# A banded attention with a squared-ReLU expert layer: the values of all head pairs in plain float32, two heads in the two column halves of the array

## The chip, the cores and the metric

The kernel runs on one core of one Trainium2 chip. The metric is the device time of one execution in microseconds (us). Of a time, three runs are shown: 820.58 us at the median, from 820.32 to 820.78.

A core has five engines with queues of their own. PE (TensorE) multiplies matrices: one operand is loaded into its array as weights (the profile calls these loads PEld), the other streams through, and the result goes to PSUM, a small memory of eight banks with 512 float32 columns each. DVE (VectorE) and ACT (ScalarE) work on SBUF and on PSUM, POOL (GpSimd) on SBUF alone, and SP issues the DMAs. An operand has up to 128 partitions (rows); "128*64 128x256" in a row of the profile says that 128 rows and 64 columns of the array are used and that the moving operand has 128 partitions and 256 columns.

## What is computed

```python
def _attn_ref(q, k, v, n_sink, window):          # q, k, v: (4, 8, 768, 64) float32
    scores = np.matmul(q, k.transpose(0, 1, 3, 2)) / np.sqrt(D)
    is_sink = pos[None, :] < n_sink               # n_sink = 4
    rel = pos[:, None] - pos[None, :]
    keep = is_sink | ((rel >= 0) & (rel < window))  # window = 128
    scores = np.where(keep, scores, -1e9)
    a = np.exp(scores - scores.max(-1)); a = a / (a.sum(-1) + 1e-9)
    return np.matmul(a, v)

x = attn_out.transpose(0, 2, 1, 3).reshape(3072, 512)
h = np.maximum(x @ w_in, 0.0)                     # w_in (512, 2048), w_out (2048, 512), float64
out = (h * h @ w_out).astype(np.float32)
```

Each query sees at most its window of 128 keys and the first four keys, the sinks.

## The kernel before

**Tiles.** The 3072 tokens are eight chunks of 384 queries, two to a batch (a first half and a second half). The eight heads go as four pairs, so there are 32 pairs of chunk and heads, numbered 0 to 31. A query block of 128 sees its own key block, the one before it and 8 sink columns that are kept beside every key block. A first-half pair has three key blocks, a second-half pair four. A key block that two query blocks see is "wide" (256 columns of queries), one that a single query block sees is "thin" (128). In a first-half pair only the last query block needs sink columns (128); in a second-half pair all three do (384).

**Two ways to multiply float32.** The format float32r goes through the array in one pass, with a rounded operand. To keep accuracy, a value is split into a rounded part and the rest (hi and lo), and the products are added up. Plain float32 needs no split and leaves two matmul records in the trace for one product. Scores of pairs 0 to 5 (`NPS`) and values of pairs 0 to 7 (`NPV`) are plain; all others, and the expert layer, go as hi and lo.

**A slot** handles the scores of pair s, the values of pair s-1 and the operands of pair s+1. `score` makes a product (L235 plain, L239 split), the masking with the maximum on DVE (L243), the exponential on ACT (L246), and at the end of a head DVE makes the reciprocal of the sums (L249, L250), POOL scales the probabilities (L253) and copies their sink columns together (L257, tile `PSk`). `sink_keys` transposes these (L265) and copies them out of PSUM. `probs` transposes the probabilities into three PSUM banks (L311): the wide blocks of head 0, the thin blocks of both heads, the wide blocks of head 1. For a split pair ACT makes the hi part (L329, L334) and DVE the rest (L330, L335); for a plain pair one copy does (L317 on DVE, L319 on ACT). `values` multiplies with v (L365) and with the sinks' v (L378 plain with 16 rows, L386 split with 48 rows). A split product has v's hi part in array columns 0 to 63 and its lo part in 64 to 127, so the upper and lower halves of the result must be added: L393 to L396. Then x is split for the expert layer (L382, L383 or L397, L398). A plain product uses columns 0 to 63 alone, for both heads, one after the other. The result tile `xo` is one PSUM bank. v of a split pair is itself split by DVE and POOL (L209, L210), the sinks' v by DVE (L180, L181).

**The expert layer** (`moe`) goes per chunk through 16 blocks of 128 hidden columns: twelve products of 384 columns into `ph` (L458), ReLU on ACT (L466, tile `r`), the square once as hi on ACT (L470, `gh`) and once in full on DVE (L471), the rest `gl` on DVE (L472). Nine products of 512 columns with w_out (L485) follow one block later, into three PSUM banks that collect all blocks of a chunk. `ph` has two banks.

**Weights** come as float64 and are turned into hi and lo on DVE, ACT and POOL by `split_part` (L542 to L554), row by row, between the other work of the first 230 us. For this the first two chunks' products go by halves of the weights.

**Order.** The program is written as one list of units. A planner (the tile framework) turns it into the queue of each engine by the order of the text, its priorities and estimated costs; a block under `tc.manual_schedule` keeps the written order on the named engines. Each engine then works through its queue in order and waits at semaphores. In slots without expert products before them (pairs 0 to 4) the attention goes beside the weights; then each step of the expert layer is followed by its share of attention units. After chunk 1 the attention pauses while weights are split, and chunk 7's expert products have no attention beside them.

The lines below have the numbers that the profile uses.

Of the kernel before, what the change touches and what calls it, by code (L numbers as in the profile page):

```python
# [18 lines left out]
P = 128  # L19
D = 64          # head size  # L20
NS = 8          # key columns that the banded path keeps for the sinks
BS = P + NS     # stride of a key block in the split keys
BAND = 2 * P + NS
TOK = 384       # queries of a chunk
# [5 lines left out]
TOP_MAX = 2.0**16 * (2.0 - 2.0**-3 - 2.0**-23)   # upper words of float64, read as float32:  # L30
TOP_MIN = 2.0**-15 * 1.125                       # what float32 can hold lies between
# [8 lines left out]
def sink_window_attention_moe(  # L40
# [26 lines left out]
    with ExitStack() as fast:  # L67
# [65 lines left out]
        # (a row of 512 float64 words becomes 512 words of hi and 512 of lo in its place)  # L133
# [13 lines left out]
        SK = wp.tile([48, TOK], F32R, name="SK")  # L147
        nc.gpsimd.memset(f32(SK), 0.0)
# [5 lines left out]
        def load_pair(c, p):  # L154
# [7 lines left out]
            if c * NPAIR + p < NPV:  # L162
                vn = ap2.tile([P, 4, 2, D], F32, tag="VV", name=f"vn_{c}_{p}")
            else:
                vn = ap1.tile([P, 4, 2, D], F32, tag="vn", name=f"vn_{c}_{p}")
# [10 lines left out]
        def load_sinks(b):  # L176
            vsn = mp.tile([48, NPAIR, 2, D], F32, tag="ob", name=f"vsn_{b}")
            nc.sync.dma_start(out=vsn, in_=vs[b])
            VS = ap1.tile([48, NPAIR, 2, 2, D], F32R, tag="VS", name=f"VS_{b}")
            nc.vector.tensor_copy(VS[:, :, :, 0, :], vsn)  # L180
            nc.vector.tensor_tensor(VS[:, :, :, 1, :], vsn, f32(VS[:, :, :, 0, :]), op=ALU.subtract)  # L181
            state["s", b] = dict(VS=VS)

        NPS, NPV = 6, 8
# [18 lines left out]
        def prep_v(c, p):  # L203
            st = state[c, p]
            if c * NPAIR + p < NPV:
                return
            nk = st["nk"]
            st["VV"] = VV = ap2.tile([P, 4, 2, 2, D], F32R, tag="VV", name=f"VV_{c}_{p}")
            nc.vector.tensor_copy(VV[:, 0:nk, :, 0, :], st["vn"][:, 0:nk])  # L209
            nc.gpsimd.tensor_tensor(  # L210
                VV[:, 0:nk, :, 1, :], st["vn"][:, 0:nk], f32(VV[:, 0:nk, :, 0, :]), op=ALU.subtract
            )

        def score(c, p, hh, i):
# [3 lines left out]
            if hh == 0 and i == 0:  # L218
                st["PSk"] = ap2.tile([P, NQ, 2, NS], F32, tag="PSk", name=f"PSk_{c}_{p}")
                st["P"], st["sm"] = [], []  # L220
# [26 lines left out]
            if i == NQ - 1:  # L247
# [9 lines left out]
                nc.gpsimd.tensor_copy(st["PSk"][:, i0:NQ, hh, :], Pt[:, i0:NQ, P:BS])  # L257

        def sink_keys(c, p):
            st = state[c, p]  # L260
# [3 lines left out]
            for i in range(i0, NQ):  # L264
                nc.tensor.transpose(  # L265
                    pss[0 : 2 * NS, (i - i0) * P : (i - i0 + 1) * P],
                    st["PSk"][:, i].rearrange("p h n -> p (h n)"), ident,
                )
            if c * NPAIR + p < NPV:
                st["SF"] = SF = ap1.tile([2 * NS, TOK], F32, tag="xs", name=f"SF_{c}_{p}")  # L270
                nc.vector.tensor_copy(SF[:, 0:nsq], pss[0 : 2 * NS, 0:nsq])
                return
            nc.scalar.copy(SK[0 : 2 * NS, 0:nsq], pss[0 : 2 * NS, 0:nsq])
            nc.vector.tensor_tensor(
# [21 lines left out]
        def probs(c, p, bi):  # L296
# [25 lines left out]
            if bi == 1:  # L322
                # hi and lo of a block that has the last queries go in one product
                tiles = [PTH]
                if used > 2 * P:
                    tiles.append(ap2.tile([P, 512], F32R, tag="PTL", name=f"PTL_{c}_{p}_{bi}"))
# [536 lines left out]
```

## Time and profile before

| | |
|---|---|
| time, median of three runs | 820.58 us |
| span of the profiled execution | 827.0 us |
| PE busy | 774.1 us (94%) |
| PE weight loads | 644.5 us (78%) |
| DVE busy | 555.9 us (67%) |
| ACT busy | 426.5 us (52%) |
| POOL busy | 323.5 us (39%) |
| mean granted PE clock | 0.968 |

The profiled execution is another one than the timed runs. The profile gives its span, from the first to the last instruction, and no other time of its own; the span stands 6.4 us above the median of the timed runs. "Busy" counts the time in which at least one instruction of the engine runs; since matmuls are pipelined, a busy PE need not be PE at its peak. A row of a group reads: line, engine, operation, result<-operands, shapes, how many | busy us, mean ns of one | idle time of the engine just before them, and what ended it. A row of stages gives the busy time and the number of instructions of each engine, then the granted PE clock as a share of full speed, the DMA share and the DMA rate.

### The profile page before, as it was taken

The numbers are of one execution on the slowest core, as the hardware profiler recorded it, in microseconds if no ns is written. First come the engines' busy times: TensorE is split into PE (matmuls) and PEld (weight loads), VectorE is DVE, ScalarE is ACT, GpSimd is POOL, SyncE is SP. The second block draws the span as 40 slices with busy tenths as digits, with TensorE's granted clock in tenths as the row PEclk, the third lists the DMA queues.
The fourth block names the chain that finished last, engine by engine and source line by source line (L and its number), as shares of the span: only waits on it lengthen the run. The fifth ranks groups of instructions, "written<-read, shape, count | busy, mean of one in ns | idle before, by whom it ended". The sixth has DMA issues, their size and how long they took to land.

```text
span 827.0 us, 11778 instructions
## 1 busy us (share of the span) xinstructions
PE 774.1 (94%) x3970; PEld 644.5 (78%) x3970; DVE 555.9 (67%) x1272; ACT 426.5 (52%) x1074; POOL 323.5 (39%) x404
## 2 busy tenths in 40 slices
PE   4979989978899899999999999999999999999996
PEld 2434567667787788988888888898888889888995
DVE  6665866898868777766766687767776776653222
ACT  5654665567455555554545565554555445442221
POOL 4553665553634453444333344443334432310000
PEclk9975899998999999999999999999999999999998
DMA  7444632354414222111201121112112220001001
GB/s 232 169 148 138 181 130 74 138 209 169 138 34 133 62 66 89 41 40 38 69 24 48 50 86 48 40 40 65 53 50 50 50 76 14 1 0 39 1 1 42
DMA packets 32644, 63.61 MB, mean 77 GB/s; under 512 B 4000, under 2 KB 13728, under 8 KB 32576
## 3 DMA queue, kind: packets, MB, share of 16 engines
q1 hardware_dynamic: 32576, 62.78, 24.1%
q8 instruction: 33, 0.54, 0.2%
q14 instruction: 35, 0.29, 0.1%
HBM read 46.52 MB, written 7.86 MB: 66 GB/s over the span
## 4 chain that ended last, share of the span: by engine, by line
PE 65%; DVE 21%; issue 4%; ACT 4%; POOL 3%; DMA 1%; SPq 0%; DVEq 0%; POOLq 0%; ACTq 0%
PE ph L458 24%; PE po L485 22%; PE xo L365 5%; PE pt L311 4%; DVE gl L472 3%; PE s L239 3%; DVE r L471 3%; PE s L235 2%; POOL P L253 2%; DVE QS L194 2%; DVE P L243 2%; DVE rs L249 1%; DVE t L543 1%; PE xo L386 1%; DVE t L542 1%
## 5 line engine op out<-in xcount | busy, mean ns | idle before, releaser
L458 PE MATMUL ph<-x,wi 128*128 128x384 f32 x1536 | 322.0, 347 | 0.3 <-POOL x L398 0.3
L458 PEld LDWEIGHTS ph<-x,wi 128*128 128x128 f32 x1536 | 267.0, 191 | 15.0 <-issue 6.7
L485 PE MATMUL po<-wo,gh 128*128 128x512 f32 x768 | 250.3, 406 | 2.6 <-DVE ob L506 2.3
L253 POOL TENSOR_SCALAR P<-P,rs 128x264 f32<-128x264 f32 (+1 forms) x192 | 116.9, 624 | 137.3 <-DVE rs L250 128.0
L471 DVE TENSOR_TENSOR r<-r 128x384 f32<-128x384 f32 x128 | 106.3, 831 | 90.8 <-ACT gh L470 90.1
L485 PE MATMUL po<-wo,gl 128*128 128x512 f32 x384 | 153.5, 400 | 10.1 <-DVE gl L472 10.0
L246 ACT ACTIVATE P<-P,nbs 128x264 f32<-128x264 f32 (+1 forms) x192 | 94.8, 494 | 126.4 <-DVE nbs L243 124.4
L485 PEld LDWEIGHTS po<-wo,gh 128*128 128x128 f32 x768 | 133.5, 190 | 23.2 <-issue 4.0
L201 POOL TENSOR_TENSOR KS<-kn,KS 128x1088 fp32r<-128x1088 f32 (+1 forms) x26 | 61.4, 2363 | 181.8 <-DVE rs L250 162.7
L466 ACT ACTIVATE r<-ph 128x384 f32<-128x384 f32 x128 | 62.5, 488 | 94.5 <-PE ph L458 94.0
L485 PEld LDWEIGHTS po<-wo,gl 128*128 128x128 f32 x384 | 72.7, 189 | 29.9 <-DVE gl L472 13.8
L472 DVE TENSOR_TENSOR gl<-r,gh 128x384 fp32r<-128x384 f32 x128 | 92.4, 722 | 4.4 <-DVE r L471 0.5
L243 DVE CUSTOM_DVE_ANT_0 P<-s,maskA 128x264 f32<-128x264 f32 x128 | 54.5, 427 | 34.0 <-PE s L239 22.1
L239 PE MATMUL s<-KS,QS 128*128 128x264 f32 (+1 forms) x312 | 64.9, 289 | 7.9 <-DVE nbs L243 3.2
L239 PEld LDWEIGHTS s<-KS,QS 128*128 128x128 f32 x312 | 55.9, 189 | 19.5 <-DVE nbs L243 5.8
L470 ACT ACTIVATE gh<-r 128x384 fp32r<-128x384 f32 x128 | 67.1, 524 | 5.8 <-POOL wo L554 2.4
L393 ACT COPY xs<-xo 64x512 f32<-64x512 f32 x48 | 28.0, 584 | 68.6 <-PE xo L386 68.3
L311 PE MATMUL pt<-ident,P 128*128 128x128 f32 x352 | 58.8, 287 | 1.1 <-DVE nbs L243 0.6
L311 PEld LDWEIGHTS pt<-ident,P 128*128 128x128 f32 x352 | 44.9, 146 | 12.5 <-POOL P L253 2.2
L394 DVE TENSOR_TENSOR xs<-xo,xs 64x512 f32<-64x512 f32 x48 | 32.8, 684 | 25.7 <-ACT xs L393 25.1
L335 DVE TENSOR_TENSOR PTL<-pt,PTH 128x512 fp32r<-128x512 f32 x48 | 33.1, 689 | 23.2 <-ACT PTH L334 22.8
L546 POOL TENSOR_SCALAR m<-raw 128x512 uint16<-128x512 uint16 x32 | 30.2, 947 | 28.7 <-PE pt L311 8.6
(102 smaller groups left out, 908.4 us busy)
## 6 DMA issues: line engine op xcount, KB each, us to landing
raw<-in_moe_w_in_dram SPq DMA_DIRECT2D x16, 512.0 KB, 3.8
raw<-in_moe_w_out_dram SPq DMA_DIRECT2D x16, 512.0 KB, 3.9
kn<-in_k_dram SPq DMA_DIRECT2D x28, 272.0 KB, 4.0
qn<-in_q_dram SPq DMA_DIRECT2D x32, 192.0 KB, 2.3
out_dram<-ob SPq DMA_DIRECT2D x24, 256.0 KB, 2.0
kn<-in_k_dram SPq DMA_DIRECT2D x24, 204.0 KB, 3.3
wi<-t SPq DMA_DIRECT2D x16, 256.0 KB, 2.5
wo<-t SPq DMA_DIRECT2D x16, 256.0 KB, 2.3
```

The costliest lines, as they stand in the source:

```text
L201: nc.gpsimd.tensor_tensor(KS[:, :, 1, 0:nk], st["kn"][:, :, 0:nk], f32(KS[:, :, 0, 0:nk]), op=ALU.subtract)
L239: nc.tensor.matmul(ps[:, 0:n], st["QS"][:, hh, qcols], flat[:, a, c0 : c0 + n], start=(a == 0), stop=(a == 1))
L243: nc.vector.tensor_tensor_reduce(Pt[:, i, 0:n], ps[:, 0:n], mask[:, 0:n], -SCALE, BIG, ALU.add, ALU.min, nb)
L246: nc.scalar.activation(Pt[:, i, 0:n], Pt[:, i, 0:n], AF.Exp, bias=nb, scale=-1.0, accum_out=sm[:, i : i + 1])
L253: nc.gpsimd.tensor_scalar(Pt[:, j, 0:n], Pt[:, j, 0:n], rs[:, j : j + 1], 1.0, op0=ALU.mult, op1=ALU.mult)
L311: nc.tensor.transpose(pt[:, off + j * P : off + (j + 1) * P], st["P"][hh][:, i, c0 : c0 + P], ident)
L458: nc.tensor.matmul(ph[:, 0:TOK], wi_at(i, cc, fc), xt[:, cc, :], start=(m == 0), stop=(m == 3 * NCC - 1),)
L466: nc.scalar.activation(r, ph[:, 0:TOK], AF.Relu)
L470: nc.scalar.activation(gh, r, AF.Square)
L471: nc.vector.tensor_tensor(r, r, r, op=ALU.mult)
L472: nc.vector.tensor_tensor(gl, r, f32(gh), op=ALU.subtract)
L485: nc.tensor.matmul(po[t], gt[:, ts_], wo[f][:, i, :], start=(f == f0 and j == 0), stop=(f == f1 - 1 and j == 2),)
```

## The change

There are five parts.

1. **Values plain for all pairs.** v and the transposed probabilities are no longer split (`prep_v`, the PTH/PTL tiles and `NPV` go); a bank of probabilities is copied once, bank 1 by DVE and the others by ACT.
2. **Two heads in two column halves.** `values` is called once per pair, after all three banks. It writes head 0 to partitions 0 to 63 and head 1 to 64 to 127 of one PSUM bank, with the products of the two heads taking turns in the written order, which PE's queue keeps. Then ACT and DVE make both parts of x for the whole pair in one operation each. The sums over the halves go.
3. **Sink rows padded to 128.** `PSK`, `SF` and the sinks' v (`VSF`, one tile for each of two batches in turn) are tiles of 128 partitions, cleared once by POOL; only the first 16 rows or columns are ever filled. The sink transposes take 128 columns in place of 16, and the sink product 128 rows in place of 16 or 48. `PSK` and `SF` exist once for all pairs. The sinks' v of a batch is loaded during the chunk before.
4. **The expert's square in the PSUM bank.** DVE multiplies `ph` by `r` in place in PSUM, ACT copies the hi part from there, DVE subtracts it.
5. **Buffers.** `vn` and the copied probabilities take three buffers each; the weight splits use these places and two of their own.

```diff
-        SK = wp.tile([48, TOK], F32R, name="SK")
-        nc.gpsimd.memset(f32(SK), 0.0)
+        SF = wp.tile([P, TOK], F32, name="SF")
+        VSF = [wp.tile([P, NPAIR, 2, D], F32, name=f"VSF{i}") for i in range(2)]
+        PSK = wp.tile([P, NQ, P], F32, name="PSK")
+        for t in (SF, *VSF, PSK):
+            nc.gpsimd.memset(t, 0.0)
...
-            vsn = mp.tile([48, NPAIR, 2, D], F32, tag="ob", name=f"vsn_{b}")
-            nc.sync.dma_start(out=vsn, in_=vs[b])
-            VS = ap1.tile([48, NPAIR, 2, 2, D], F32R, tag="VS", name=f"VS_{b}")
-            nc.vector.tensor_copy(VS[:, :, :, 0, :], vsn)
-            nc.vector.tensor_tensor(VS[:, :, :, 1, :], vsn, f32(VS[:, :, :, 0, :]), op=ALU.subtract)
+            nc.sync.dma_start(out=VSF[b % 2][0 : 2 * NS], in_=vs[b])
...
-                nc.gpsimd.tensor_copy(st["PSk"][:, i0:NQ, hh, :], Pt[:, i0:NQ, P:BS])
+                nc.gpsimd.tensor_copy(PSK[:, i0:NQ, hh * NS : hh * NS + NS], Pt[:, i0:NQ, P:BS])
...
+                nc.tensor.transpose(pss[:, (i - i0) * P : (i - i0 + 1) * P], PSK[:, i], ident)
+            nc.vector.tensor_copy(SF[0 : 2 * NS, 0:nsq], pss[0 : 2 * NS, 0:nsq])
...
+            st["PT"][bi] = PTF = ap3.tile([P, 512], F32, tag="PTF", name=f"PTF_{c}_{p}_{bi}")
             if bi == 1:
+                nc.vector.tensor_copy(PTF[:, 0:used], pt[:, 0:used])
+            else:
+                nc.scalar.copy(PTF[:, 0:used], pt[:, 0:used])
+
+        def values(c, p):
+
             st = state[c, p]
+            i0 = 2 if c % NHALF == 0 else 0
             nsq = (NQ - i0) * P
+            xo = ps_x.tile([P, 512], F32, tag="xo", name=f"xo_{c}_{p}")
+            todo = ([], [])
+            for bi in (2, 1, 0):
+                for h, kk, qs, off in st["banks"][bi][0]:
+                    n = len(qs) * P
+                    todo[h].append((slice(qs[0] * P, qs[0] * P + n), st["vn"][:, kk, h, :], st["PT"][bi][:, off : off + n]))
+            for h in range(2):
+                todo[h].append((slice(i0 * P, TOK), VSF[c // NHALF % 2][:, p, h, :], SF[:, 0:nsq]))
+            last = len(todo[0]) - 1
+            with tc.manual_schedule(engines={mybir.EngineType.PE}):
+                for n in range(last + 1):
+                    for h in (1, 0):
+                        cols, lhsT, rhs = todo[h][n]
+                        nc.tensor.matmul(
+                            xo[h * D : h * D + D, cols], lhsT, rhs, start=(n == 0), stop=(n == last), skip_group_check=True
+                        )
...
+            nc.scalar.copy(xh[:, p, :], xo[:, 0:TOK])
+            nc.vector.tensor_tensor(xl[:, p, :], xo[:, 0:TOK], f32(xh[:, p, :]), op=ALU.subtract)
...
-                lambda: probs(*a, 0), lambda: sink_keys(*a), lambda: values(*a, 0, 0),
-                lambda: probs(*a, 1), lambda: values(*a, 1, 0), lambda: probs(*a, 2),
-                lambda: values(*a, 1, 1), lambda: values(*a, 2, 1),
+                lambda: probs(*a, 0), lambda: sink_keys(*a), lambda: probs(*a, 1), lambda: probs(*a, 2),
+                lambda: values(*a),
...
-                    sc[0], va[0], sc[1], va[1], sc[2], va[3], va[2], sc[3], va[5], sc[4], va[4], sc[5],
-                    pr[0], pr[1], va[6], pr[2], va[7],
+                    sc[0], va[0], sc[1], va[1], sc[2], va[2], sc[3], va[3], sc[4], va[4], sc[5],
+                    pr[0], pr[1], pr[2],
...
-                    nc.scalar.activation(gh, r, AF.Square)
-                    nc.vector.tensor_tensor(r, r, r, op=ALU.mult)
-                    nc.vector.tensor_tensor(gl, r, f32(gh), op=ALU.subtract)
+                    nc.vector.tensor_tensor(ph[:, 0:TOK], ph[:, 0:TOK], r, op=ALU.mult)
+                    nc.scalar.copy(gh, ph[:, 0:TOK])
+                    nc.vector.tensor_tensor(gl, ph[:, 0:TOK], f32(gh), op=ALU.subtract)
```

The host's layout of the sinks' v loses its second copy of 16 rows.

More of the change, by code (lines that the diff above doesn't have):

```diff
@@ L264, in sink_keys @@
             for i in range(i0, NQ):
[L265 to L274, printed above, removed]
-                SK[32 : 32 + 2 * NS, 0:nsq], pss[0 : 2 * NS, 0:nsq], f32(SK[0 : 2 * NS, 0:nsq]), op=ALU.subtract
-            )
+                nc.tensor.transpose(pss[:, (i - i0) * P : (i - i0 + 1) * P], PSK[:, i], ident)
+            nc.vector.tensor_copy(SF[0 : 2 * NS, 0:nsq], pss[0 : 2 * NS, 0:nsq])
         def banks_of(c, p):
@@ L301, in probs @@
                 st["PT"] = {}
-                st["xo"] = {}
-                st["left"] = [st["nk"]] * 2
             bank, used = st["banks"][bi]
@@ L313, in probs @@
                     )
-            if c * NPAIR + p < NPV:
-                st["PT"][bi] = PTF = ap2.tile([P, 512], F32, tag="PTH", name=f"PTF_{c}_{p}_{bi}")
-                if bi == 1:
-                    nc.vector.tensor_copy(PTF[:, 0:used], pt[:, 0:used])
-                else:
-                    nc.scalar.copy(PTF[:, 0:used], pt[:, 0:used])
-                return
-            PTH = ap2.tile([P, 512], F32R, tag="PTH", name=f"PTH_{c}_{p}_{bi}")
-            if bi == 1:
-                tiles = [PTH]
-                if used > 2 * P:
-                    tiles.append(ap2.tile([P, 512], F32R, tag="PTL", name=f"PTL_{c}_{p}_{bi}"))
-                for n, t in enumerate(tiles):
-                    src = pt[:, n * 2 * P : (n + 1) * 2 * P]
-                    nc.scalar.copy(t[:, 0 : 2 * P], src)
-                    nc.vector.tensor_tensor(t[:, 2 * P :], src, f32(t[:, 0 : 2 * P]), op=ALU.subtract)
-                st["PT"][bi] = [t.rearrange("p (t h c) -> p t h c", t=2, h=2) for t in tiles]
-                return
@@ L333, in probs @@
-            PTL = ap2.tile([P, 512], F32R, tag="PTL", name=f"PTL_{c}_{p}_{bi}")
-            nc.scalar.copy(PTH[:, 0:used], pt[:, 0:used])
-            nc.vector.tensor_tensor(PTL[:, 0:used], pt[:, 0:used], f32(PTH[:, 0:used]), op=ALU.subtract)
-            st["PT"][bi] = (PTH, PTL)
-        def values(c, p, bi, hh):
+            st["PT"][bi] = PTF = ap3.tile([P, 512], F32, tag="PTF", name=f"PTF_{c}_{p}_{bi}")
+            if bi == 1:
+                nc.vector.tensor_copy(PTF[:, 0:used], pt[:, 0:used])
+            else:
+                nc.scalar.copy(PTF[:, 0:used], pt[:, 0:used])
@@ L496, in evacuate @@
             for t in range(NQ):
-                pool, tag = (ap2, "PTH") if c == NCHUNK - 1 and t == 2 else (mp, "ob")
+                pool, tag = (ap3, "PTF") if c == NCHUNK - 1 and t == 2 else (mp, "ob")
                 ob = pool.tile([P, DM], F32, tag=tag, name=f"ob_{c}_{f0}_{t}")
@@ L575, in sink_window_attention_moe @@
             load_row(n)
-        vsf = ap1.tile([2 * NS, NPAIR, 2, D], F32, tag="VS", name="vsf")
-        nc.sync.dma_start(out=vsf, in_=vs[0, 0 : 2 * NS])
-        state["vsf"] = vsf
+        load_sinks(0)
         start_pair(1)
@@ L826, in layouts @@
     sinks = np.broadcast_to(kt[:, :, :, None, :NS], (B, H, D, nb, NS))
-    vs = np.zeros((B, 48, H // 2, 2, D), v.dtype)
-    for r0 in (0, 32):
-        for t in range(2):
-            vs[:, r0 + t * NS : r0 + t * NS + NS, :, t, :] = v[:, t::2, 0:NS].transpose(0, 2, 1, 3)
+    vs = np.zeros((B, 2 * NS, H // 2, 2, D), v.dtype)
+    for t in range(2):
+        vs[:, t * NS : t * NS + NS, :, t, :] = v[:, t::2, 0:NS].transpose(0, 2, 1, 3)
     arrays = {
```

87 lines of the change are left out of this document (9 added, 78 removed).

## The prediction

> **What bounds the kernel now.** I read the page first, then busy time by stage, then groups, then single stretches of PE.
>
> ```profile
> span 827.0 us, 11778 instructions
> PE 774.1 (94%) x3970; PEld 644.5 (78%) x3970; DVE 555.9 (67%) x1272; ACT 426.5 (52%) x1074; POOL 323.5 (39%) x404
> ...
> PEclk9975899998999999999999999999999999999998
> ```
> ```profile
> core 0: us, PE busy (x) PEld busy (x) DVE busy (x) ACT busy (x) POOL busy (x), PEclk, DMA share, GB/s
> 0.00:36.00 36.00, 23.09 (x64) 11.87 (x65) 22.82 (x87) 20.23 (x57) 20.30 (x35) 1.00 0.60 196
> 36.00:75.00 39.00, 34.00 (x107) 17.08 (x106) 22.57 (x68) 21.94 (x66) 18.19 (x29) 0.69 0.50 170
> 75.00:150.00 75.00, 70.38 (x316) 46.94 (x317) 50.54 (x120) 42.51 (x110) 41.58 (x50) 0.89 0.38 116
> 150.00:200.00 50.00, 39.97 (x172) 32.41 (x173) 48.89 (x70) 34.75 (x87) 28.88 (x24) 0.94 0.58 209
> 200.00:230.00 30.00, 27.58 (x144) 24.28 (x144) 22.77 (x57) 16.04 (x42) 12.47 (x14) 0.99 0.30 95
> 230.00:750.00 520.00, 510.08 (x2830) 450.08 (x2829) 367.00 (x836) 273.58 (x681) 202.11 (x254) 1.00 0.17 50
> 750.00:827.00 77.00, 69.04 (x345) 61.86 (x343) 21.32 (x38) 17.47 (x34) 0.00 (x0) 0.97 0.06 22
> ```
>
> Four regimes are to be seen. From 230 to 750 us, 63% of the span, PE is busy 98% of the time: only PE time counts. From 150 to 200 it is DVE (48.89 of 50 us). Up to 150 PE is busy most of the time, but it waits for others too, and its clock is only 0.69 in one stretch. The last 77 us are expert products alone. The profiled execution is put against its own span, 827.0; the three timed runs have a median of 820.58, 6.4 below it. I take every saving as equal in both.
>
> **Term 1: the values of the split pairs, 230 to 750 us (pairs 8 to 31).** What they cost, and how PE pays for changes of its array shape (a row begins with its start and its length in us; x4 merges four records):
>
> ```profile
> 609.86 0.28 PE L365 MATMUL xo<-PTH,VV 128*128 128x256 f32 x1
> 609.97 0.28 PE L365 MATMUL xo<-PTL,VV 128*128 128x256 f32 x1
> 610.09 0.28 PE L365 MATMUL xo<-PTH,VV 128*128 128x256 f32 x1
> 610.21 0.28 PE L365 MATMUL xo<-PTL,VV 128*128 128x256 f32 x1
> 610.41 0.32 PE L386 MATMUL xo<-SK,VS 48*128 48x128 f32 x1
> 610.67 1.31 PE L458 MATMUL ph<-x,wi 128*128 128x384 f32 x6
> ...
> 110.86 1.22 PE L458 MATMUL ph<-x,wi 128*128 128x384 f32 x6
> 112.01 0.65 PE L365 MATMUL xo<-PTF,vn 128*64 128x128 f32 x4
> 112.59 0.85 PE L378 MATMUL xo<-SF,vsf 16*64 16x384 f32 x2
> 113.38 0.51 PE L239 MATMUL s<-KS,QS 128*128 128x264 f32 x2
> ```
> ```profile
> L311 PE MATMUL pt<-ident,P 128*128 128x128 f32 x260 | 40.0, 272 | 0.0
> L365 PE MATMUL xo<-PTH,VV 128*128 128x256 f32 x144 | 38.3, 282 | 0.0
> L365 PE MATMUL xo<-PTL,VV 128*128 128x256 f32 x96 | 24.8, 280 | 0.0
> L265 PE MATMUL pss<-ident,PSk 128*16 128x128 f32 x47 | 8.8, 271 | 5.9 <-DVE PTL L335 5.1 <-DVE nbs L243 0.8
> L365 PE MATMUL xo<-PTL,VV 128*128 128x128 f32 x48 | 8.2, 250 | 0.0
> L386 PE MATMUL xo<-SK,VS 48*128 48x128 f32 x24 | 7.8, 323 | 0.0
> ```
>
> Matmuls overlap, so I count from start to start or end to end. A split product of 256 columns takes 0.12 us (609.97 to 610.09), one of 128 half of that. The sink product of 48 rows ends at 610.73, 0.24 after the product before it, of which 0.06 is work: 0.18 to go in. The six ph products behind it end 1.25 later; six without a change take 6 x 0.175 = 1.05 (384 columns at the same rate): 0.20 to get out. I count the 24 sink products of 384 columns (0.175 of work) the same way. Now: 240 x 0.12 + 48 x 0.06 + 24 x (0.06 + 0.175) + 48 x 0.38 = 28.8 + 2.9 + 5.6 + 18.2 = 55.5 us.
>
> A plain float32 product leaves two records. In the fence below two records of 256 columns last 0.65 (83.59) and four 1.08 (35.77), so one more is 0.215: 0.43 per product of 256 columns, 0.215 per 128 and 0.645 per 384. Going into the 64-column shape costs 0.14 (from 112.08 to 112.66 is 0.58 for 0.44 of work), a further 0.14 for 16 rows (112.66 to 113.44 is 0.78 for 0.645), coming out 0.21 (113.44 to 113.89 is 0.45 for 0.24).
>
> ```profile
> 35.77 1.08 PE L365 MATMUL xo<-PTF,vn 128*64 128x256 f32 x4
> ...
> 72.10 1.25 PE L235 MATMUL s<-kn,qn 64*128 64x264 f32 x2
> ...
> 77.77 1.25 PE L235 MATMUL s<-kn,qn 64*128 64x264 f32 x4
> ...
> 83.59 0.65 PE L365 MATMUL xo<-PTF,vn 128*64 128x256 f32 x2
> 85.23 0.65 PE L365 MATMUL xo<-PTF,vn 128*64 128x256 f32 x2
> ```
>
> Per head a second-half pair has two wide blocks, two thin ones and 384 sink columns: 0.86 + 0.43 + 0.645 = 1.935. A first-half pair has two wide, one thin and 128: 1.29. If both heads run at once, one change in and out is added (0.35): 2.285 and 1.64. Twelve of each: 47.1 us, so **-8.4 us**. No row shows two column halves at work together; that is the unknown cost. The nearest row is on row halves: at 77.77 four float32 records of two heads take 1.25 us, as long as the two records of one head at 72.10. That is full overlap, and I take it. The far bound is none: 12 x (2 x 1.935 + 0.35 + 2 x 1.29 + 0.35) = 85.8, **+30.3**.
>
> On this the Trainium skill (TensorE: Matmul & The Clock Gate, "What overlaps and what doesn't") says that matmuls start and end strictly in program order. The trace disagrees: with the two passes of a head issued together, four records would take three passes, and the row at 77.77 shows two. If the rule held for column halves, it gives the lockstep rival below.
>
> The sink transposes stay at three or one per pair, now of 128 columns; a 16-column one (271 ns) already takes what a full one does (272), so nothing. Their 5.9 us of waiting, 5.1 of it for the subtraction that frees a PSUM bank, shrink: that subtraction is gone and one copy frees the bank. I take **-3** (0 to -6).
>
> **Term 2: the square, and DVE at 150 to 200 us.**
>
> ```profile
> L542 DVE TENSOR_SCALAR t<-raw 128x512 int32<-128x512 int32 x14 | 12.4, 888 | 0.1
> ...
> L471 DVE TENSOR_TENSOR r<-r 128x384 f32<-128x384 f32 x8 | 6.8, 846 | 0.0
> L472 DVE TENSOR_TENSOR gl<-r,gh 128x384 fp32r<-128x384 f32 x7 | 5.8, 830 | 0.0
> ```
> ```profile
> L335 DVE TENSOR_TENSOR PTL<-pt,PTH 128x512 fp32r<-128x512 f32 x48 | 33.1, 689 | 23.2 <-ACT PTH L334 22.8
> L383 DVE TENSOR_TENSOR x<-xo,x 64x384 fp32r<-64x384 f32 x16 | 8.8, 549 | 8.1 <-ACT x L382 7.9
> ```
> ```profile
> L471 DVE TENSOR_TENSOR r<-r 128x384 f32<-128x384 f32 x17 | 10.0, 587 | 43.4 <-ACT gh L470 43.4
> ```
>
> The first fence is of 150 to 200 us: both operations on SBUF operands take some 840 ns. The last is the tail, where POOL is idle: 587. So about 250 ns is contention. An operation with one operand in PSUM takes 549 for 384 columns. No row writes PSUM from DVE; I bound it by 549 and by 689 (the 512-column row) and take 549, the same length. Eight items save 8 x (0.846 + 0.830 - 1.098) = 4.6 us; at 689, 2.4. I take **-4** (0 to -7; more than 4.6 where the items around 200 to 230 gain too; nothing if the row splits, still 14 x 0.888 and more, wait for ACT instead). From 230 on the saving is off the path and I give it nothing. The new chain goes ACT, DVE, ACT, DVE, as long as the old one, where the square on DVE already waited for ACT (43.4 us above). The bank of ph is now held until the last subtraction, but the po products that need its result come before its next user. ACT copies gh out of PSUM where it squared; not on the path at 52% busy.
>
> **Term 3: pairs 0 to 7, already plain.** Their heads go one after the other, with the shape changed at least four times per pair (83.59 and 85.23 are two visits for one head). Now per second-half pair 2 x 1.935 + 4 x 0.35 + 2 x 0.14 = 5.55, later 2.285: -3.3, four pairs, -13 us, all at 75 to 150. There PE is busy 94%, but DVE does 50.54 of 75 and many of its results are awaited: I take **-8** (-3 to -13). First-half pairs: 2 x 1.29 + 1.68 = 4.26 to 1.64, four pairs, -10.5, more at the lower clock of 36 to 75. Up to 75 PE has 18 us idle and the splits, masks and DMAs set much of the pace: **-4** (0 to -12).
>
> **What is moved or waits anew, at no cost.** All products of a pair now stand in one block on PE, which needs the third PTF copy and SF. Behind it stand ph, po and scores. A score and a step of the expert layer lie between the transposes and the block and cover the copy; without that cover it is one 512-column evacuation (0.69, L335) per pair, 24 pairs, +17 us at the worst. PSK and SF exist once: the POOL copy of the next pair waits for transposes that PE has issued a score earlier. The sink values come by one SP transfer per batch, in the third slot of the chunk before; SP's queue then holds only loads for the next pairs. Their splits, those of v, and the sums and subtraction of x leave ACT, DVE and POOL, idle enough after 230. Four clears on POOL at the start replace one, at some 0.4 us each in a stage where it idles 16 of 36 us.
>
> ```profile
> L148 POOL MEMSET SK<- 48x384 f32 x1 | 0.4, 412 | 0.0
> ```
>
> **Sum.** -8.4 - 3 - 4 - 8 - 4 = -27.4: span 799.6, time 820.6 - 27.4 = **793**.
>
> **Rivals.**
> *Start not set by PE:* term 3 hides behind splits and DMA. For it: DVE waits and the 0.69 clock; against: 94% at 75 to 150. -8.4 - 3 - 4 = -15.4: 805.
> *Lockstep:* the halves overlap only in order, so each step takes the longer of its two products: 4 x 0.43 + 0.645 + 0.35 = 2.715 and 3 x 0.43 + 0.215 + 0.35 = 1.855 per pair. Term 1 becomes 12 x 4.57 - 55.5 = -0.7, term 3 about -10 in place of -12: -0.7 - 3 - 4 - 10 = -17.7: 803. The row at 77.77 speaks against it.
> *No overlap (slower):* the column halves of one shape take turns, since both stream all 128 rows, which the row halves do not. Term 1 is +30.3; pairs 0 to 7 save only three changes and the sink's (1.33 each, 10.6, I take 6). 30.3 - 3 - 4 - 6 = +17: 838. It decides from where less than about 40% of the second head is hidden: the second head is 12 x (1.935 + 1.29) = 38.7 and the gains without overlap net only 21.
> *All of it:* every term at its bound, -8.4 - 6 - 7 - 13 - 12 = -46: 774.
>
> **Chances.** Forecast 0.45, with its own range 782 to 806; start hidden 0.22; lockstep 0.12; no overlap 0.12; all of it 0.09. A range of 770 to 818 leaves out no overlap and little at the lower end. This kernel's runs differ by 0.06%, so 0.2% (1.6 us) can be told from no change. Faster 0.85 (all but no overlap, less a little for a lost cover), same 0.03, slower 0.12.
>
> **What would show it.** Right: in a block on PE, records of the two heads start a few ns apart, and ten second-half products fill 1.9 us, not 3.9; ph behind the block starts 0.2 late once per pair instead of twice; the DVE square takes about 550 at every stage; 230 to 750 shrinks by about 11 us and everything before 150 by about 12. Wrong: records of the second head that start only when the first's end; new waits of PE for PTF or SF ahead of the block; DVE on PSUM far above 689.

## The result, and the profile after

The changed kernel takes 799.74 us at the median of four runs (798.45 to 801.20); the kernel before took 820.68 in the same series (820.32 to 820.78 in three runs, 834.83 in a fourth). The ratio is 0.974, with a 95% interval of 0.970 to 0.977. A second series of four gave 801.18 and 0.975 (0.971 to 0.978). The forecast was 793 with a range of 770 to 818: the sign and the range held, and the gain is 20.9 us where 27.6 were forecast.

From the page of the kernel after: span and engines, and the groups of the square (L389) and the query split (L190).

```profile
span 796.7 us, 11779 instructions
PE 737.8 (93%) x4066; PEld 618.8 (78%) x4066; DVE 453.6 (57%) x1126; ACT 369.8 (46%) x958; POOL 245.9 (31%) x359
...
L389 DVE TENSOR_TENSOR ph<-ph,r 128x384 f32<-128x384 f32 x128 | 71.8, 561 | 74.8 <-ACT r L385 74.1
...
L190 DVE TENSOR_TENSOR QS<-qn,QS 64x384 fp32r<-64x384 f32 x52 | 47.9, 921 | 1.6
```

PE lost 36 us of busy time, DVE 102, ACT 57 and POOL 78, and PE still sets the pace at 93%. The square takes 561 ns in the mean of the whole span. The query split, which the change does not touch, now takes 921 (604 before).

To see where the time went I cut both spans by work, at the last copy of a chunk's output out of PSUM: the start (up to the first half of chunk 0's output), the middle (its second half and both halves of chunk 1), the chunks 2 to 6, and the rest (70.7 us before, 70.0 after). Busy time by the first three stages, first of the kernel before, then after; the columns are stage, length, busy us and instructions of PE, PEld, DVE, ACT and POOL, granted clock, DMA share and rate.

```profile
0.00:168.20 168.20, 141.45 (x546) 85.94 (x546) 113.93 (x302) 97.22 (x262) 91.38 (x122) 0.88 0.47 152
168.20:314.10 145.90, 131.70 (x687) 114.37 (x687) 116.73 (x250) 84.09 (x219) 67.85 (x79) 0.98 0.35 115
314.10:756.30 442.20, 438.26 (x2427) 388.19 (x2428) 307.07 (x691) 229.41 (x567) 164.30 (x204) 1.00 0.16 45
```
```profile
0.00:151.80 151.80, 114.44 (x544) 77.90 (x544) 105.71 (x292) 93.57 (x256) 87.33 (x123) 0.92 0.53 170
151.80:288.10 136.30, 127.81 (x710) 110.48 (x711) 94.71 (x227) 75.64 (x197) 54.91 (x71) 0.99 0.38 121
288.10:726.70 438.60, 433.76 (x2509) 375.04 (x2506) 234.99 (x579) 185.94 (x477) 103.65 (x166) 1.00 0.16 46
```

The start is 16.4 us shorter, the middle 9.6, the five chunks 3.6 and the rest 0.7: 30.3 together, 9.4 more than the medians differ by. Part of that is the execution that the profile of before had caught (first experiment). The surprise is the five chunks: they are more than half of the span and PE's own, and gave only 3.6 us. PE's busy time there fell by 4.5, and its idle time (length less busy) rose from 3.9 to 4.8. The waits of PE in the whole span of the kernel after (us in total, times, longest) show two that grew by more than 2 us, for POOL's copy `PSK` (5.4 before) and for POOL's key subtraction `KS` (2.6 before), and a new one of that size, for the rounded square `gh`, of which 4.1 us lie in the five chunks:

```profile
PE pss L248 <- POOL PSK L241: 13.4, 6, 3.6
PE s L223 <- POOL KS L197: 8.7, 6, 2.0
...
PE po L404 <- ACT gh L390: 6.3, 10, 1.8
```

And this is one block of a second-half pair on PE in the timeline of the kernel after (start, length; xN merges records):

```profile
464.73 0.40 PE L404 MATMUL po<-wo,gl 128*128 128x512 f32 x1
465.05 1.57 PE L309 MATMUL xo<-PTF,vn 128*64 128x256 f32 x16
466.40 0.86 PE L309 MATMUL xo<-SF,VSF 128*64 128x384 f32 x4
```

From the end of the product before it (465.13) to the end of the last sink record (467.26) are 2.13 us for the twenty records of two heads; forecast were 0.14 to go in and 1.935. The first records of the two heads start 7 ns apart.

### The profile page after: what moved, and what is told of

Its sections match the earlier page's. It is cut to its first block, busy times and chain, and to the rows that moved or that the text cites. A ratio compares the mean times of both kernels' runs of the same rounds, so it can differ in the third digit from the quotient of the medians.

```text
span 796.7 us, 11779 instructions
## 1 busy us (share of the span) xinstructions
PE 737.8 (93%) x4066; PEld 618.8 (78%) x4066; DVE 453.6 (57%) x1126; ACT 369.8 (46%) x958; POOL 245.9 (31%) x359
## 4 chain that ended last, share of the span: by engine, by line
PE 66%; DVE 10%; POOL 4%; ACT 4%; issue 3%; DVEq 0%; POOLq 0%; ACTq 0%
PE po L404 26%; PE ph L377 26%; PE xo L309 6%; PE s L223 4%; PE pt L282 4%; DVE rs L233 3%; POOL KS L197 2%; ACT P L230 1%; DVE KS L196 1%; DVE QS L190 1%; DVE t L462 1%; ACT gh L390 1%; DVE ph L389 1%; PE pss L248 1%; POOL wo L473 1%
## 5 line engine op out<-in xcount | busy, mean ns | idle before, releaser
L377 PE MATMUL ph<-x,wi 128*128 128x384 f32 x1536 | 313.4, 344 | 0.0
L377 PEld LDWEIGHTS ph<-x,wi 128*128 128x128 f32 x1536 | 266.0, 189 | 17.9 <-issue 9.4
L237 POOL TENSOR_SCALAR P<-P,rs 128x264 f32<-128x264 f32 (+1 forms) x192 | 91.4, 492 | 214.5 <-DVE rs L234 165.3
L197 POOL TENSOR_TENSOR KS<-kn,KS 128x1088 fp32r<-128x1088 f32 (+1 forms) x26 | 65.8, 2531 | 190.0 <-DVE KS L196 79.9
L389 DVE TENSOR_TENSOR ph<-ph,r 128x384 f32<-128x384 f32 x128 | 71.8, 561 | 74.8 <-ACT r L385 74.1
L390 ACT CAST gh<-ph 128x384 fp32r<-128x384 f32 x128 | 60.7, 474 | 88.7 <-DVE ph L389 85.0
L391 DVE TENSOR_TENSOR gl<-ph,gh 128x384 fp32r<-128x384 f32 x128 | 71.1, 555 | 47.5 <-ACT gh L390 47.4
L309 PE MATMUL xo<-PTF,vn 128*64 128x256 f32 x448 | 50.3, 366 | 0.0
L318 DVE TENSOR_TENSOR x<-xo,x 128x384 fp32r<-128x384 f32 x32 | 17.8, 556 | 55.2 <-ACT x L317 55.2
L190 DVE TENSOR_TENSOR QS<-qn,QS 64x384 fp32r<-64x384 f32 x52 | 47.9, 921 | 1.6
L309 PEld LDWEIGHTS xo<-PTF,vn 128*64 128x64 f32 x448 | 33.5, 145 | 19.6 <-issue 9.6
```

Of the source, the lines that this page charges most:

```text
L197: nc.gpsimd.tensor_tensor(KS[:, :, 1, 0:nk], st["kn"][:, :, 0:nk], f32(KS[:, :, 0, 0:nk]), op=ALU.subtract)
L237: nc.gpsimd.tensor_scalar(Pt[:, j, 0:n], Pt[:, j, 0:n], rs[:, j : j + 1], 1.0, op0=ALU.mult, op1=ALU.mult)
L309: nc.tensor.matmul(xo[h * D : h * D + D, cols], lhsT, rhs, start=(n == 0), stop=(n == last), skip_group_check=True)
L377: nc.tensor.matmul(ph[:, 0:TOK], wi_at(i, cc, fc), xt[:, cc, :], start=(m == 0), stop=(m == 3 * NCC - 1),)
L389: nc.vector.tensor_tensor(ph[:, 0:TOK], ph[:, 0:TOK], r, op=ALU.mult)
L390: nc.scalar.copy(gh, ph[:, 0:TOK])
```

## The experiments

Each run is compared with runs of the kernel before on the same chip. "The five chunks" are chunks 2 to 6, cut as above.

**The kernel before once more.**

> The kernel before, unchanged, profiled once more. Its first profile has a span of 827.0 us, the changed kernel's 796.7: 30.3 apart, where the medians are 20.9 apart. Theory: the first profile caught an execution some 8 us longer than the median (a time is a span and 1.75 us in the changed kernel's runs); then this one has a span near 819 and the difference lies where the two profiles of the same kernel differ. Rival: the kernel before has a span above its time; then the span is 827 again.

It took 825.93 us, with a span of 824.1, not the 819 that was expected: this execution was a long one too. In every run with both numbers the time is 1.7 to 1.9 above the span, never below it. So the profiled execution of before, with its span of 827.0, must have taken about 828.8 and was a long one, 8 us above the median. The kernel before scatters: 818.83 to 829.04 in the seven runs beside this one, and up to 834.83 in all series. The 0.06% of the prediction came from three runs and was far too small. Cut by work, this run has its start at 166.2 (168.2 in the first profile), and no other piece differs by more than 0.7. As far as two profiles can show it, both of long executions, the scatter is in the start.

**The square alone.** The kernel before, with part 4 only:

```diff
-                    nc.scalar.activation(gh, r, AF.Square)
-                    nc.vector.tensor_tensor(r, r, r, op=ALU.mult)
-                    nc.vector.tensor_tensor(gl, r, f32(gh), op=ALU.subtract)
+                    nc.vector.tensor_tensor(ph[:, 0:TOK], ph[:, 0:TOK], r, op=ALU.mult)
+                    nc.scalar.copy(gh, ph[:, 0:TOK])
+                    nc.vector.tensor_tensor(gl, ph[:, 0:TOK], f32(gh), op=ALU.subtract)
```

> The kernel before with the expert's square made in the PSUM bank and nothing else. By the prediction's term 2: -4 us (0 to -7), 816.5, gained at 150 to 200 us alone. Rival, from the changed kernel's profile: gh now comes after a DVE operation and PE's po products wait for it, about 2 us per chunk in 6 chunks; then the gain at 150 to 200 is paid back later, 820 to 828.

809.56 us (807.96 to 810.36), ratio 0.982 (0.975 to 0.989): 14 us, not 4. In the groups of DVE from 311 to 739 us, which are most of the five chunks in both, first the full square of the kernel before (in the run above), then the square and the sums before the reciprocal of this one; last the five chunks by stage:

```profile
L471 DVE TENSOR_TENSOR r<-r 128x384 f32<-128x384 f32 x76 | 69.3, 911 | 34.9 <-ACT gh L470 34.2
```
```profile
L470 DVE TENSOR_TENSOR ph<-ph,r 128x384 f32<-128x384 f32 x77 | 43.1, 560 | 23.0 <-ACT r L466 22.6
...
L249 DVE TENSOR_SCALAR rs<-sm 128x3 f32<-128x3 f32 x36 | 20.8, 578 | 6.8 <-ACT P L246 6.3
```
```profile
300.40:739.00 438.60, 437.65 (x2429) 388.50 (x2428) 278.67 (x690) 225.17 (x567) 146.60 (x204) 1.00 0.17 46
```

The contention that I had read at 150 to 200 us (840 ns) was stronger still in the five chunks, 911. With the operand in PSUM the square is free of it at every stage (556 to 563 ns). Part of it went elsewhere: the sums take 578 ns where they took 228, the query split 612 where it took 553. PE's busy time is that of before (437.65 against 438.26), but its idle time falls from 3.9 to 0.95: 3.6 us off the five chunks that I had given nothing. The middle is 6.0 shorter, the start 5.7 to 7.7 (of which its scatter may be a part).

On this the Trainium skill (SBUF — State Buffer, "Who interferes with whom") says that a DVE instruction with two SBUF inputs contends with a GpSimd one that reads SBUF, and one with at most one SBUF input, outside the two-port modes, does not. The trace agrees: 911 against 560.

**The values alone.** The kernel after, with the three lines of the square as they were before.

> The changed kernel with the old square (ACT squares r, DVE squares r in SBUF). By the prediction: the values alone, -23 of -27, so about 4 us slower than the changed kernel, 804. Rival: the new chain of the square costs PE about 2 us per chunk; then this is faster than the changed kernel, 790 to 797, with no wait of po for ACT gh.

814.01 us (810.85 to 815.73), ratio 0.989 (0.982 to 0.996): slower than either case of the expectation, and 10 us faster than the kernel before where 23 were forecast for the values. The five chunks by stage, and three groups of DVE in 288 to 727 us: the square, the query split, and the sums before the reciprocal.

```profile
302.10:738.80 436.70, 432.57 (x2508) 375.45 (x2505) 242.10 (x577) 190.33 (x478) 118.58 (x166) 1.00 0.17 46
```
```profile
L390 DVE TENSOR_TENSOR r<-r 128x384 f32<-128x384 f32 x80 | 45.8, 573 | 51.8 <-ACT gh L389 51.8
...
L190 DVE TENSOR_TENSOR QS<-qn,QS 64x384 fp32r<-64x384 f32 x37 | 33.6, 909 | 1.2
...
L233 DVE TENSOR_SCALAR rs<-sm 128x3 f32<-128x3 f32 x39 | 28.0, 719 | 2.8 <-ACT P L230 0.7 <-issue 0.4
```

PE's work falls by 5.7 us in the five chunks, where Term 1 gives 20 of 24 pairs, 7.0. But the expected end of its waits does not come: idle 4.1, of which 2.9 us are waits for the rest `gl`. The contention has moved: the square on SBUF runs at 573 ns, nearly alone, and the query split takes 909 instead of 553, the little operation on three columns 719 instead of 228 (the groups of before are shown with the keys, below). The sums were slow with the square alone too; the query split is slow, to this degree, only where the values are plain. In the five chunks the two parts alone are worth 3.6 and 5.5 us, and both together 3.6. Over the whole time the intervals are too wide to tell whether they add up.

**The rounded square from `r`.** The kernel after, with the hi part made from SBUF, beside DVE's square rather than behind it:

```diff
-                    nc.scalar.copy(gh, ph[:, 0:TOK])
+                    nc.scalar.activation(gh, r, AF.Square)
```

> The changed kernel, but ACT makes gh as the square of r at once, beside the DVE multiplication in PSUM, so gh no longer waits for DVE. If the wait for gh is what took back the gain: -10 to -14 us against the changed kernel, 786 to 790. If the wait only moves on to gl: 797 to 800.

792.37 us (791.30 to 794.46), ratio 0.963 (0.956 to 0.970): 7 to 9 us below the two medians of the changed kernel. The five chunks by stage:

```profile
286.60:720.20 433.60, 432.07 (x2510) 375.64 (x2507) 239.37 (x578) 190.63 (x478) 104.46 (x166) 1.00 0.17 46
```

PE idles 1.5 us there, not 4.8, and the five chunks are 8.6 shorter than before, close to the 9.1 of the two parts added. So the new chain is not "as long as the old one" where it counts. The query split still takes 974 ns in this kernel, as in the kernel after: only the wait behind it is gone. Why only some items wait is to be seen in a stretch of the kernel after (timeline, all engines; in brackets the idle time before and what ended it):

```profile
493.04 2.85 POOL L197 TENSOR_TENSOR KS<-kn,KS 128x1088 fp32r<-128x1088 f32 x1 [9.05 <-DVE KS L196]
...
493.41 0.47 ACT L385 ACTIVATE r<-ph 128x384 f32<-128x384 f32 x1
...
493.61 2.31 DVE L233 TENSOR_SCALAR rs<-sm 128x3 f32<-128x3 f32 x1
...
496.62 0.54 DVE L389 TENSOR_TENSOR ph<-ph,r 128x384 f32<-128x384 f32 x1
...
497.20 0.48 ACT L390 CAST gh<-ph 128x384 fp32r<-128x384 f32 x1 [3.32 <-DVE ph L389]
...
497.73 0.73 PE L404 MATMUL po<-wo,gh 128*128 128x512 f32 x2 [0.48 <-ACT gh L390]
```

POOL's key subtraction starts at 493.04. DVE's operation on three columns, which starts after it, lasts until 495.92, 0.03 after POOL is done. `r` is ready at 493.88, but its square starts at 496.62, the rounded copy only at 497.20, and PE stands for 0.48. With `gh` made from `r` on ACT, the copy need not wait for DVE.

**The kernel after once more**, for its scatter and beside the next three.

> The changed kernel, unchanged, as the base of the three runs beside it: 800 us.

801.18 us (800.86 to 802.40). The start takes 151.7 (151.8 in the first profile of this kernel), the five chunks 438.5 (438.6). The middle takes 139.1 (136.3), with the granted clock at 0.95 (0.99): so a difference of 3 us in the middle can be scatter.

**No overlap.** Each product of the kernel after with the 128 columns of both heads as weights, written to all partitions:

```diff
-                    todo[h].append((slice(qs[0] * P, qs[0] * P + n), st["vn"][:, kk, h, :], st["PT"][bi][:, off : off + n]))
+                    todo[h].append((slice(qs[0] * P, qs[0] * P + n), st["vn"][:, kk].rearrange("p t d -> p (t d)"), st["PT"][bi][:, off : off + n]))
...
-                            xo[h * D : h * D + D, cols], lhsT, rhs, start=(n == 0), stop=(n == last), skip_group_check=True
+                        nc.tensor.matmul(xo[:, cols], lhsT, rhs, start=(n == 0 and h == 1), stop=(n == last), skip_group_check=True)
```

> The changed kernel with the weights of both heads (128 columns) in every product of the block, written to all 128 partitions, so that nothing can overlap and the shape of the array never changes; what one head adds to the other's rows makes the output another one than the reference's. If overlap works as predicted (2.07 us per second-half pair and 1.58 per first-half pair with the change of shape, against 3.87 and 2.58): +1.8 and +1.0 per pair, +34 us over the 24 later pairs, up to +11 for the first eight: 830 to 845. If the values are hidden anyway: 800.

837.53 us (836.81 to 842.75), ratio 1.020 (1.015 to 1.025), 36 above the kernel after. A second-half block in the timeline, and the five chunks by stage:

```profile
487.70 0.39 PE L402 MATMUL po<-wo,gl 128*128 128x512 f32 x1
487.93 2.78 PE L309 MATMUL xo<-PTF,vn 128*128 128x256 f32 x16
490.55 1.45 PE L309 MATMUL xo<-SF,VSF 128*128 128x384 f32 x4
```
```profile
301.10:766.30 465.20, 460.31 (x2515) 408.99 (x2513) 235.11 (x578) 185.93 (x477) 103.64 (x166) 1.00 0.16 43
```

The block takes 3.91 us (488.09 to 492.00) instead of 2.13: without overlap ten products fill 3.9, as the far bound of Term 1 had it (2 x 1.935 = 3.87). In the five chunks PE's busy time grows by 26.5. So the whole gain of the values, and more, is the overlap.

**Head by head.** The same products with the two loops exchanged:

```diff
-                for n in range(last + 1):
-                    for h in (1, 0):
+                for h in (1, 0):
+                    for n in range(last + 1):
```

> The changed kernel with all products of head 1 issued before those of head 0. If the column halves work from queues that look far ahead: no change, 800. If only neighbours in the order overlap: the heads go one after the other, 830 to 845 as without overlap, less little.

832.95 us (830.42 to 833.27), ratio 1.012 (1.008 to 1.016). A block in the timeline:

```profile
486.61 0.39 PE L404 MATMUL po<-wo,gl 128*128 128x512 f32 x1
486.93 1.57 PE L309 MATMUL xo<-PTF,vn 128*64 128x256 f32 x10
488.28 0.49 PE L309 MATMUL xo<-SF,VSF 128*64 128x384 f32 x1
488.34 0.60 PE L309 MATMUL xo<-PTF,vn 128*64 128x128 f32 x3
488.60 0.49 PE L309 MATMUL xo<-SF,VSF 128*64 128x384 f32 x1
...
489.42 0.81 PE L309 MATMUL xo<-SF,VSF 128*64 128x384 f32 x2
```

It takes 3.23 us (487.00 to 490.23). The halves overlap only where their products stand near each other in the queue. Head 1 has eight records from `PTF`; ten start before its first sink record at 488.28, so at least two of head 0 ran ahead of it, though they stand behind both of head 1's sink records. In this block the seventh and the eighth record start 6 ns apart (488.06), which reads as head 0's first beside the seventh of head 1's ten: the reach is some four records here. So the order "taking turns" carries 32 us.

This bears on the rule on program order weighed in the prediction (the Trainium skill, TensorE: Matmul & The Clock Gate, "What overlaps and what doesn't"): the trace disagrees with strict order of starts for column halves too, by these ten records.

**Sink rows not padded.** The sink product of the kernel after over the 16 rows that are filled:

```diff
-                todo[h].append((slice(i0 * P, TOK), VSF[c // NHALF % 2][:, p, h, :], SF[:, 0:nsq]))
+                todo[h].append((slice(i0 * P, TOK), VSF[c // NHALF % 2][0 : 2 * NS, p, h, :], SF[0 : 2 * NS, 0:nsq]))
```

> The changed kernel with the sink products on 16 rows, as the plain pairs had it before. By the 0.14 us that a change to 16 rows took in the profile of before, once per pair: 32 x 0.14 = +4.5 us, 804; if each head's sink product changes the shape for itself or overlap ends there, up to 0.14 + 0.64 per pair: +15. If the padding does nothing: 800.

811.36 us (806.73 to 813.39), ratio 0.985 (0.980 to 0.989). The end of a block in the timeline:

```profile
476.34 0.39 PE L404 MATMUL po<-wo,gl 128*128 128x512 f32 x1
476.66 1.56 PE L309 MATMUL xo<-PTF,vn 128*64 128x256 f32 x16
478.16 0.86 PE L309 MATMUL xo<-SF,VSF 16*64 16x384 f32 x4
```

It takes 2.29 us (476.73 to 479.02), 0.16 more, near the 0.14 that the prediction counted for this change of shape; the overlap goes on. Over 20 pairs that is 3.2 of the 5.0 us that the five chunks grow by. The start grows by 9.6, far more than eight pairs at 0.16. There PE's clock is another one. The start by stage, and the plain scores in it, by groups: first of this kernel, then of the kernel after.

```profile
0.00:161.40 161.40, 132.31 (x544) 87.48 (x544) 104.08 (x292) 94.12 (x256) 87.60 (x123) 0.85 0.51 159
```
```profile
L219 PE MATMUL s<-kn,qn 64*128 64x264 f32 x56 | 31.6, 715 | 1.7 <-DVE nbs L227 1.7
```
```profile
L219 PE MATMUL s<-kn,qn 64*128 64x264 f32 x56 | 25.0, 576 | 1.9 <-DVE nbs L227 1.9
```

The granted clock is 0.85 in the mean against 0.92 (0.50 throughout from 60 to 100 us), and the same 56 records last 715 ns instead of 576. The four runs of this kernel go with it roughly: 806.73 us at a mean clock of 0.977, 810.17 at 0.973, 813.39 at 0.965 and 812.55 at 0.960. How much of the 10 us the padding itself is worth can be said only for the five chunks.

**The keys on DVE.** The subtraction that collides, moved from POOL to DVE:

```diff
-            nc.gpsimd.tensor_tensor(KS[:, :, 1, 0:nk], st["kn"][:, :, 0:nk], f32(KS[:, :, 0, 0:nk]), op=ALU.subtract)
+            nc.vector.tensor_tensor(KS[:, :, 1, 0:nk], st["kn"][:, :, 0:nk], f32(KS[:, :, 0, 0:nk]), op=ALU.subtract)
```

> The changed kernel with the rest of the keys (KS) subtracted by DVE in place of POOL. In the changed kernel POOL's KS runs beside DVE's work on SBUF operands: QS takes 974 ns (553 before), and a 3-element rs 2.31 us beside a KS of 2.85 us; the square behind them is late, and PE waits 0.75 us for gh. If that collision is the cause of the wait: QS back to about 550, rs to about 170, no wait of po for gh between 290 and 720, 4 to 8 us faster than the changed kernel, 793 to 797. If the cause is only that the prep operations stand together ahead of the square: DVE has 1.2 us more per pair there, and it is the same or slower, 800 to 806.

785.91 us (785.03 to 787.04), ratio 0.954 (0.947 to 0.960): 14 to 15 us below the kernel after, more than expected. The query split and the sums, by groups over the five chunks: first the kernel before, then after, then this one with its key subtraction; last its five chunks by stage.

```profile
L194 DVE TENSOR_TENSOR QS<-qn,QS 64x384 fp32r<-64x384 f32 x36 | 19.9, 553 | 1.1
...
L249 DVE TENSOR_SCALAR rs<-sm 128x3 f32<-128x3 f32 x37 | 8.5, 228 | 3.5 <-ACT P L246 2.9
```
```profile
L190 DVE TENSOR_TENSOR QS<-qn,QS 64x384 fp32r<-64x384 f32 x36 | 35.1, 974 | 1.1
...
L233 DVE TENSOR_SCALAR rs<-sm 128x3 f32<-128x3 f32 x37 | 23.3, 630 | 5.6 <-ACT P L230 4.3
```
```profile
L190 DVE TENSOR_TENSOR QS<-qn,QS 64x384 fp32r<-64x384 f32 x36 | 20.0, 554 | 1.3 <-issue 0.2
...
L233 DVE TENSOR_SCALAR rs<-sm 128x3 f32<-128x3 f32 x37 | 6.2, 169 | 5.5 <-ACT P L230 4.2
...
L197 DVE TENSOR_TENSOR KS<-kn,KS 128x1088 fp32r<-128x1088 f32 x10 | 14.0, 1396 | 0.0
```
```profile
282.70:715.70 433.00, 431.03 (x2510) 376.54 (x2506) 223.06 (x597) 187.08 (x477) 72.78 (x148) 1.00 0.16 46
```

The subtraction takes 1.4 us on DVE where it took 2.85 on POOL in the stretch above, and DVE, with that work added, is busy for 12 us less in the five chunks (223.06 against 234.99). The query split is back at 554 ns from 974, the sums are at 169 from 630. In the five chunks PE waits no more for `gh`: its idle time there is 2.0 us, and they are 9.2 shorter than before. So the collision is what makes the chain late there.

The five chunks are 5.6 us shorter than in the kernel after, so most of the 14 to 15 us lies elsewhere. One candidate is in the waits of PE in the whole span: for the key subtraction itself it waited 8.7 us in the kernel after (shown above), nearly all of it before the five chunks, and waits 3.6 here.

```profile
PE s L223 <- DVE KS L197: 3.6, 6, 1.3
```

No run takes this apart from the collision.

**Both repairs.** Keys on DVE and `gh` from `r`.

> The same with gh made by ACT from r. If the collision causes the waits for gl that were left with gh from r (0.3 to 0.7 us about once per pair): 4 to 6 us faster than that kernel's 792: 786 to 789. If the square's chain and the collision cost the same wait: no gain over either alone, 792.

785.41 us (784.41 to 786.75), ratio 0.953 (0.946 to 0.960): the same as the keys on DVE. In the five chunks the collision and the longer chain are not two losses but one wait, which either repair takes away (433.6 with `gh` from `r`, 433.0 with the keys on DVE, 432.4 with both). Outside them the keys on DVE are worth some 6 us more, and `gh` from `r` adds nothing to that.

**The sinks last.** On top of `gh` from `r`, the sink transposes behind the third bank of probabilities, to cover the wait of 13.4 us for POOL's copy `PSK`:

```diff
-                lambda: probs(*a, 0), lambda: sink_keys(*a), lambda: probs(*a, 1), lambda: probs(*a, 2),
+                lambda: probs(*a, 0), lambda: probs(*a, 1), lambda: probs(*a, 2), lambda: sink_keys(*a),
```

> The changed kernel with gh from r and the sink transposes behind the third bank of probabilities instead of behind the first. Up to 150 us PE waits 15 to 30 us for POOL's copy of the sink columns. If that wait sets the start: the first output leg, 153 us, shortens by 5 to 10, 782 to 787. If POOL's scaling of the probabilities is late next, PE waits for that instead: 792.

805.27 us (803.76 to 806.47), ratio 0.977 (0.970 to 0.984): 13 above the kernel that it was made from. The start takes 163.6 in place of 153.1, the middle 136.5 in place of 133.5, the five chunks 434.4 in place of 433.6. It was to be faster or the same. The start by stage:

```profile
0.00:163.60 163.60, 130.18 (x544) 86.06 (x544) 103.07 (x292) 95.00 (x258) 88.12 (x123) 0.79 0.50 158
```

PE's wait for `PSK` fell to 7.8 us, and 2.6 of new waiting for POOL's scaling came. But PE is busy for 15 us more than in the start of the kernel it was made from (115.09), with two instructions more, at a clock of 0.79, and the plain scores last 691 ns there instead of 584. What the shorter wait gave, the slower PE took. The mean clock of a run does not tell this, though: of the four runs of this kernel two show 0.951 (805.95 and 806.47 us) and two 0.990 (803.76 and 804.58). The next run shows how that can be.

**All three.**

> gh from r, keys on DVE and the sink transposes last, together. If all three causes are as stated and do not overlap: 778 to 783, faster than each. If the start's wait only moves: 786 to 789.

797.05 us (793.96 to 800.20), ratio 0.966 (0.959 to 0.974), slower than both cases of the expectation. The start is 162.0 again. Its plain scores, by groups, and two stretches of PE with them:

```profile
L219 PE MATMUL s<-kn,qn 64*128 64x264 f32 x56 | 30.8, 698 | 1.7 <-DVE nbs L227 1.7
```
```profile
50.76 1.25 PE L219 MATMUL s<-kn,qn 64*128 64x264 f32 x2
...
97.66 0.71 PE L219 MATMUL s<-kn,qn 64*128 64x264 f32 x2
```

They are as slow as with 16 sink rows (715), though the stages of this run give the start a clock of 0.99. Two records take 1.25 us at 50.76, as long as the two at 72.10 in the prediction's fence, where the kernel before has its granted clock at 0.50; at 97.66 two take 0.71. In this run every one of these 264-column records up to 92 us lasts 641 ns or more, and the four behind that 382 or 487. In the kernel before the scores up to 30 us last 641 to 807 ns as well, in a stage whose clock is given as 1.00. So a clock of 1.00 in the stages of the start is no sign that PE ran at full speed. By the durations PE was slow here up to some 95 us.

## Why the prediction was right, and where it was off

**The sum and its base.** The terms made 27.4 us, and the two profiles differ by 30.3. That the sum came so near is luck in part. With the square alone 14 us (9 to 20) are gained where Term 2 has 4, and with the values alone 10 (3 to 15) where the other terms have 23: errors of opposite sign. A step that missed is "I take every saving as equal in both": the span of 827.0 belonged to an execution 8 us longer than the median, and its surplus lay in the start, where Term 3 was at work. 799.6 as a span is about 801.4 as a time, near the 799.74 and 801.18 measured. I subtracted from the median savings of which some were surplus. If all the surplus lay in the start, the start gains 20.9 - 9.6 - 3.6 - 0.7 = 7.0 us against a median execution; Term 3 had 12. That is 5.0 of the 6.7 us that the forecast was too low. It is an estimate: no median execution of the kernel before was profiled, and the middle of the kernel after scatters by 2.8 us.

**Term 1, overlap.** Right. Full overlap was taken from row halves; column halves do the same: 2.13 us for a block against 2.075 forecast, 3.91 without overlap. Lockstep would have needed 2.5 (2.715 less the 0.21 to get out). "No overlap" gives 837.53 when it is forced, where that rival said 838; that the two agree to 1 us is chance, since its sum has Term 2 at 4 and changes of shape that weights of 128 columns do not have. In the kernel after no matmul of the block waits for `PTF` or `SF` (its weight loads wait 3.4 us for `PTF` in the whole span), so the cover held. PE's work in the five chunks fell by 5.7 us with the values alone, where the term gives 7.0.

**Term 1, the wait of the sink transposes.** In the five chunks the wait for the subtraction went with the splits. But PE's idle time did not fall by it: 3.9 to 4.8, because `gh` is late. In the start their wait for POOL's copy grew: 5.4 us for PE before, 13.4 after. The -3 was not gained.

**What moves at no cost.** This failed: "leave ACT, DVE and POOL, idle enough after 230". In the five chunks of the kernel before POOL's key subtractions overlap 18 of DVE's squares and 1 of its 36 query splits; in the kernel after 1 square and 25 query splits. So they came to lie beside DVE's query split and sums (553 to 974 ns, 228 to 630 ns), and the square behind them comes late. Both parts have a share: the sums are slow with the square alone, too (578). The other half of the failure is "the new chain ... as long as the old one". Together they cost 5 us in the five chunks; the two repairs give 7 to 15 in all, the larger with the shorter wait for the keys in it.

**Term 2.** 549 ns for DVE in PSUM was right (561). But "from 230 on the saving is off the path and I give it nothing" was wrong: the square alone is worth 14 us, of which 3.6 in the five chunks and 6.0 in the middle. A share of 98% for PE hid 3.9 us of idle time, of which 3.0 went with the long square.

**Term 3.** The mechanism holds in one direction: without overlap PE is busy for 13.8 us more in the start, and the start is 11.1 longer. In the other it holds in part: PE's busy time there fell by 27.0 us between the two profiles and the start by 16.4, and with the low clock of the 16 sink rows it is 17.9 more and 9.6 longer. So the rival that the start is not set by PE has fallen as a whole, but not every microsecond of PE counts. The size was off, 7.0 against a median execution for a forecast of 12, and not even the 7.0 is all Term 3's: against the two profiles of the kernel before, the start is 7.7 to 9.7 shorter with the values alone and 5.7 to 7.7 with the square alone. That a PE at half speed stretches the start, by some 10 us from one kernel or execution to another, was not in the prediction's terms. Why PE is slow for long in one of them and not in the other stays open.

**What would show it.** Blocks and the length of the square came as written. The start shrank by 16.4 between the profiles and by some 7 against a median execution, where 12 were written; the five chunks and the second half of chunk 1, about 230 to 750, shrank by 8.5 (498.7 to 490.2) instead of 11.

## What to carry to other kernels

Two products that use different column halves of the array run at once if they stand side by side in the written order: let the halves take turns, and give all of them one shape. When work is taken from an engine, look at what runs beside what afterwards: here POOL's key subtraction came to lie beside DVE's query split and sums, and moving that one line won two thirds as much again as the change. And set a sum against several executions, not against the one that the profile caught, and test its terms one by one: here terms that were wrong in opposite directions made a good sum.

## What the runs showed of the hardware that was not expected

- A DVE operation on three columns took 2.31 us while POOL's subtraction of 2.85 us ran, and 169 ns in the mean without it.
- The subtraction of 1088 columns is faster on the engine that is the busier one: 1.4 us on DVE, 2.85 on POOL, and DVE's own busy time falls by it.
- In the start the same 56 score records took from 553 to 715 ns in the mean; nearly all of them took either 382 or 487 ns or 641 to 807. In the kernels with 691 to 715 ns the start was 10 to 12 us longer than in the kernel after. In one of these (698) the stages give a clock of 0.99.
- Matmul records of one column half ran ahead of records of the other half that stand before them in the queue, by some four records in the block shown.
